# Pooled scores of one batch from every fourth column of q, and a rearranged start

## The chip, the cores and the metric

The kernel runs on one core of a Trainium2 chip. A core has five engines with a queue each: TensorE (PE in the profile; its weight loads are listed as PEld), VectorE (DVE), ScalarE (ACT), GpSimd (POOL) and SyncE (SP), which here issues nearly all DMAs. The engines run side by side and wait for each other through semaphores. Inputs and output lie in the chip's memory (HBM); work is done from an on-chip buffer, and matmul results arrive in an accumulation buffer, PSUM, of eight banks. The metric is the time of one execution in microseconds (us), as a median over runs. The profile is of one execution, and its span covers the instructions alone.

## The reference: what is computed

Shapes: q, k and v are 8 batches x 8 heads x 576 positions x 64. Two attentions are added, then a second block works on the result.

```python
q_d = q.reshape(B, H, Sd, 4, D).mean(axis=3)      # Sd = 144; k_d, v_d likewise
out_d = sm_attn(q_d, k_d, v_d)                    # softmax(q_d k_d' / 8) v_d
out_up = np.repeat(out_d, 4, axis=2)
scores = np.where(abs(i - j) < 4, scale * q @ k.T, -1e9)
out_local = softmax(scores) @ v
x = (out_up + out_local), heads side by side      # 576 x 512 per batch
theta = x @ w_theta
u = x + w_tok_r @ (x * cos(theta)) + w_tok_i @ (x * sin(theta))
return u + np.maximum(u @ w_ch, 0.0)
```

The pooled scores are the product of sums over four neighbouring positions of q and of k. Since the product is linear in q, the sum over the four positions of q may be taken before the product or after it.

## The kernel before

**One list of words sets the order.** `ORDER` is written out by hand: 1191 words, each one step of one batch (and of one part of it). The last loop reads the words in turn; the first two letters name the step, which takes the next item of its own list of batches and parts, and the rest names a place: an engine (v VectorE, a ScalarE, g GpSimd), a PSUM bank or pair of banks, or one of 16 staging buffers. `pin` ties every instruction to the one before it on its engine, so that each engine works strictly in the order of the words. Nothing is planned at run time: an engine waits at its next instruction until the data and the banks are there. While a batch is in its second block, the next batch's attention is already under way.

**The way of a batch**, with the two letters of the words. SyncE loads k and q (`lk`, `lq`, line 287) and casts bring them to bf16 (`ck`, `cq`, line 295). TensorE transposes them (`tp`, line 302) so that head dimensions lie on partitions, and `ev` (line 315) copies the result from PSUM to `kT` and `qT`. `kd` and `qd` (lines 319 to 336) sum four neighbouring columns: on VectorE one reduction (line 321), on GpSimd two additions (lines 329, 332 and 335). v comes in through `lv`, `lw`, `cv`; for batch 0 alone through whole loads, casts, transposes, copies and products with the identity (`l1`, `c1`, `t1`, `e1`, `x1`, lines 362 to 390). `pv` and `vd` make the pooled v. Then come two softmaxes side by side:

- the local one: scores of windows of 64 positions (`ps`, line 482), exponential (`ex`, 490), band mask (`mk`, 503 and 505), product with v (`po`, 515), division (`nm`, 523 and 524);
- the pooled one: scores (`sd`, line 426), exponential (`ed`, 437), product with the pooled v (`nd`, 447 and 452), division (`xn`, 457 and 458), transpose and copy (`xd`, `xc`).

`xt` transposes the local result, and `xa` (line 545) adds the two into `xT`. The second block takes `xT` through theta (`th`, line 556), sines (`cs`, 561 and 562), products (`zz`), the token mixing (`mx`, line 636, the largest piece of work), the sum (`ua`), and the channel product (`ch`, line 666) with its output (`rl`, `st`). The weights are loaded (`la`, `lb`, `lc`) and cast (`ca`, `cb`, `cc`) in between; the token weights are also transposed (`wp`, `wc`).

**The pooled scores.** `sd` fills a pair of banks in two parts of twelve matmuls each. In every one of them 64 head dimensions meet two groups of 32 pooled keys and 144 pooled queries: a 64x64 corner of the array, with 144 columns moving through it. The row half is the head's parity `par`, which also names the bank; the column half is `x`. The exponential `ed` scales by 1/8 and by 1/16, since both operands are sums of four and not means.

**Idle matmuls.** A word `wm` multiplies a buffer of zeros into a bank that nothing reads: the first figure after it is the bank, the second a count of 512-column matmuls, the third a last piece in units of 64 columns. Six more of 512 columns stand ahead of the list (line 226). In the part that is changed there are words of 7168, 1984, 960, 1088, 1280 and 2944 columns.

Of the kernel before, what the change touches and what calls it, by code (L numbers as in the profile page):

```python
# [15 lines left out]
B = 8  # L16
# [4 lines left out]
SD = S // 4  # L21
# [8 lines left out]
NCH = 5  # L30
# [9 lines left out]
HALF = 64  # L40
# [4 lines left out]

XDMA = (6, 7)
# [6 lines left out]
VT = (0,)  # L53
# [10 lines left out]
lv8 cbg wcv wcv wp1 zz zp7 tp45 cs qdg wp3 wp6 zz wcv lw zz wcv wcv zca eva wp7 wcv wp1 wca te wp0 wcv ps34 ps56 ex ex  # L64
ps12 mx0 lq1 cvg lk2 lka mx7 lqc mx3 qdv cvg ua lk7 ex ua lk0 mkv mkv kdg sd67 po45 nm sd12 lq4 cva lk5 lk9 cvg cvg ed
ed mx0 ua ua lq3 pv67 po45 po23 nm mx0 vda mkg nd67 lk8 nd45 lkb nm xn xn lq6 ckg ckg tp12 mx3 po45 ua lca ua nm cqg
cqg tp67 eva eva xd0 ckg ckg up1 lq7 po23 lvc xcv nm tp45 xt67 cqg mx0 cqg xt23 eva xt45 lv4 qdg kdg uca lw lv0 lw lw
lv3 lv1 lw lw xa xa tp67 cka ts ckg ckg th1 th2 xa th5 lk8 xm4 evv cs cqg xm1 ckv th3 zz tt4 up6 lq6 lqb cs zz tp12
xm7 ua cs ucv ct cs cqg eva te ztv xm6 zz zz mx0 ua tp34 zp7 tp56 ps12 zcv mx7 mx0 ex cvv kdg evv eva lk7 lk9 cvg lk4
qdg ua up7 uca sd12 mkv ps34 po56 ex ua ccv lcc lc5 kdg nm mkv mx0 sd34 ed po56 cvg cvg ua cqg mx7 nm ua ed mx0 ua lk2  # L70
# [30 lines left out]
def kernel(  # L101
# [11 lines left out]
    nc = tc.nc  # L113
# [28 lines left out]
    qT = tiles(2, [P, 4, S], "qT")  # L142
# [665 lines left out]
```

## Time and profile before

| | |
|---|---|
| median of 3 runs | 233.53 us (231.45, 233.53, 234.31) |
| profiled execution | 231.04 us |
| its span | 229.3 us, 9430 instructions |
| TensorE busy | 219.4 us, 96% of the span |
| VectorE, ScalarE, GpSimd busy | 187.8, 154.3 and 147.4 us |
| DMA, first 40 us | 11.62 MB, 291 GB/s on average |
| token mixing, line 636 | 576 matmuls, 78.1 us |
| pooled scores, line 426 | 192 matmuls, 5.6 us |
| idle matmuls of the list, line 764 | 32 matmuls, 9.9 us |
| pooled sums of q on GpSimd, first addition | 14 times, 16.5 us |

A row of the chain of waits gives start, length, engine, tile and line, and how many instructions are merged in it. A row of the timeline gives start, length, engine, line, operation, the tile written and the tiles read with their shapes, the count, and in brackets how long the engine stood idle before and what it waited for. In the row of the slices each digit is the busy share of one fortieth of the span, in tenths. A row of a group ends in its busy time, the mean of one instruction in ns, and the idle time ahead of it. The length of a matmul in a row holds its way through the array too; the pace of a series is read from the chain, where such overlap is taken out. A busy TensorE in the first 20 us is in part busy with idle matmuls.

### The profile page before, as it was taken

The page shows a single profiled execution, that of the slowest core. Times are in us where ns is not written, and L with a number is a line of the kernel's source. Part 1 is how long each engine was busy: PE and PEld are TensorE (multiplying, and loading weights), DVE is VectorE, ACT ScalarE, POOL GpSimd, SP SyncE. Part 2 cuts the span into 40 slices and gives each one's busy share as a digit, 9 for nine tenths or more (in the row PEclk, how much of TensorE's full clock was granted, in tenths as well). Part 3 has the DMA queues.
Part 4 walks back from the last instruction along what each step waited for, and adds up shares of the span by engine and source line. Part 5 has one row for each costly group of instructions (what it writes and reads, how often), then busy time and mean ns, then how long its engine had stood idle before and what let it go on. Part 6 is the DMA issues. An engine that isn't in the chain of part 4 may idle for free.

```text
span 229.3 us, 9430 instructions
## 1 busy us (share of the span) xinstructions
PE 219.4 (96%) x3970; PEld 152.3 (66%) x3970; DVE 187.8 (82%) x370; ACT 154.3 (67%) x240; POOL 147.4 (64%) x194
## 2 busy tenths in 40 slices
PE   7997899999999999999999999989998999999992
PEld 2475678776878666885785685766655775667741
DVE  6599998989988899889978798798986967648473
ACT  2279999689988999898888997868786132530000
POOL 7589998879996999997978399379933020200000
PEclk9999999999999999999999999999999999999999
DMA  6999987999998799979799996992473466655787
GB/s 180 394 390 390 294 176 212 370 326 174 319 336 162 196 297 265 203 163 284 157 261 353 270 146 175 136 131 77 90 152 84 71 139 186 139 146 132 152 223 268
DMA packets 76795, 49.41 MB, mean 216 GB/s; under 512 B 61136, under 2 KB 61392, under 8 KB 76752
## 3 DMA queue, kind: packets, MB, share of 16 engines
q1 hardware_dynamic: 76096, 47.76, 80.7%
q10 hardware_dynamic: 656, 1.05, 1.3%
q8 instruction: 31, 0.51, 1.0%
q14 instruction: 12, 0.10, 0.2%
HBM read 33.98 MB, written 9.44 MB: 189 GB/s over the span
## 4 chain that ended last, share of the span: by engine, by line
PE 75%; DVE 10%; DMA 5%; POOL 4%; issue 2%; ACT 2%; SPq 0%; DVEq 0%; POOLq 0%; ACTq 0%
PE PS L636 27%; PE PS L666 10%; PE PS L556 10%; PE PS L302 5%; DMA ur<-uT 4%; PE PS L515 2%; PE PS L537 2%; PE PS L595 2%; PE PS L764 2%; PE PS L482 2%; PE PS L568 2%; POOL two L329 1%; POOL pm L503 1%; PE PS L447 1%; DVE pm L505 1%
## 5 line engine op out<-in xcount | busy, mean ns | idle before, releaser
L636 PE MATMUL PS<-WT,z 128*128 128x288 bf16 x576 | 78.1, 286 | 0.0
L636 PEld LDWEIGHTS <-z 128*128 128x128 bf16 x576 | 53.9, 98 | 16.1 <-issue 1.3
L641 DVE TENSOR_TENSOR uT<-PS,xT 128x288 bf16<-128x288 f32 x64 | 28.5, 451 | 10.2 <-PE PS L636 9.4
L561 ACT ACTIVATE cs<-PS,pihc 128x512 bf16<-128x512 f32 x32 | 22.1, 690 | 21.0 <-PE PS L556 13.4
L556 PE MATMUL PS<-wth,xT 128*128 128x512 bf16 x128 | 32.1, 379 | 0.1
L666 PE MATMUL PS<-wch,uT 128*128 128x512 bf16 (+1 forms) x132 | 31.1, 373 | 0.0
L524 DVE TENSOR_TENSOR tmp<-PS,rl 128x512 bf16<-128x512 f32 x40 | 27.6, 691 | 1.4
L545 DVE TENSOR_TENSOR xT<-PS,xdT 128x928 bf16<-128x928 f32 (+1 forms) x24 | 22.3, 952 | 3.7 <-PE PS L537 3.6
L490 ACT ACTIVATE pm<-PS 128x1024 bf16<-128x1024 f32 (+1 forms) x24 | 20.5, 880 | 6.6 <-PE PS L482 5.4
L674 DVE SCALAR_TENSOR_TENSOR osb<-PS,ur 128x512 f32<-128x512 f32 x28 | 19.1, 685 | 6.7 <-DMA ur<-uT 3.9
L577 POOL TENSOR_TENSOR zT<-xT,cst 128x512 bf16<-128x512 bf16 x7 | 10.0, 1422 | 21.8 <-ACT cst L574 21.8
L295 POOL CAST k_tm<-st 128x576 bf16<-128x576 f32 x23 | 15.5, 691 | 7.6 <-DMA st<-in_k_dram 7.5
L770 ACT ACT_TABLE_LOAD x15 | 19.2, 1283 | 0.3
L666 PEld LDWEIGHTS <-uT 128*128 128x128 bf16 x132 | 11.9, 98 | 11.2
L295 POOL CAST q_tm<-st 128x576 bf16<-128x576 f32 x24 | 17.0, 725 | 3.3 <-DMA st<-in_q_dram 3.2
L562 ACT ACTIVATE cs<-PS 128x512 bf16<-128x512 f32 x32 | 19.1, 598 | 0.0
L396 POOL CAST v_w<-st 128x512 bf16<-128x512 f32 x21 | 13.4, 656 | 8.5 <-DMA st<-in_v_dram 8.5
L556 PEld LDWEIGHTS <-xT 128*128 128x128 bf16 x128 | 11.4, 98 | 10.3 <-DVE xT L545 0.7
L503 POOL TENSOR_TENSOR pm<-pm,band 128x512 bf16<-128x512 bf16 x16 | 18.1, 1158 | 0.0
L329 POOL TENSOR_TENSOR two<-qT 128x576 f32<-128x576 bf16 x14 | 16.5, 1177 | 1.5 <-ACT qT L315 1.2
L620 DVE TENSOR_TENSOR z<-PS,cs 128x1024 bf16<-128x1024 bf16 x24 | 15.8, 683 | 0.8 <-issue 0.4
L329 POOL TENSOR_TENSOR two<-kT 128x580 f32<-128x580 bf16 x13 | 15.0, 1154 | 0.4
(123 smaller groups left out, 421.5 us busy)
## 6 DMA issues: line engine op xcount, KB each, us to landing
st<-in_k_dram SPq DMA_DIRECT2D x32, 288.0 KB, 6.2
st<-in_q_dram SPq DMA_DIRECT2D x32, 288.0 KB, 5.8
st<-in_v_dram SPq DMA_DIRECT2D x70, 128.0 KB, 4.9
out_dram<-osb SPq DMA_DIRECT2D x26, 256.0 KB, 3.5
st<-in_v_dram SPq DMA_DIRECT2D x4, 288.0 KB, 3.0
st<-in_moe_w_tok_r_dram SPq DMA_DIRECT2D x4, 288.0 KB, 6.2
st<-in_moe_w_tok_i_dram SPq DMA_DIRECT2D x4, 288.0 KB, 6.0
st<-in_moe_w_theta_dram SPq DMA_DIRECT2D x4, 256.0 KB, 5.9
```

The costliest lines, as they stand in the source:

```text
L295: COPY[w](out=to, in_=of)
L329: nc.gpsimd.tensor_tensor(out=t, in0=src[:, :, 0:2], in1=src[:, :, 2:4], op=ALU.add)
L490: nc.scalar.activation(out=pm[(3 * b + u) % NPM][:, :, 0:n].rearrange("p e c j w -> p e (c j w)"), in_=at.pop(("ps", b, u))[:, :, 0:4 * W ...
L503: EW[w].tensor_tensor(out=t[:, x], in0=t[:, x], in1=m[:, x], op=ALU.mult)
L524: nc.vector.tensor_tensor(out=tmp[(NCH * b + c) % NTMP].rearrange("p g (j d) -> p g j d", d=D), in0=ps[:, :, :, 0:D], in1=r.unsqueeze(3).t ...
L545: nc.vector.tensor_tensor(out=xT[b % 2][:, :, lo:lo + cnt].rearrange("p e (m j) -> p e m j", j=4), in0=at.pop(("xt", b, u))[:, :, 0:cnt].r ...
L556: nc.tensor.matmul(out=ps, lhsT=xT[b % 2][:, dc, P * c:P * c + P], rhs=wth[:, dc, :], start=(dc == 0), stop=(dc == 3))
L561: nc.scalar.activation(out=t[:, 0, :], in_=ps, func=AF.Sin, bias=pihc, scale=1.0)
L636: nc.tensor.matmul(out=ps, lhsT=z[b % 2][:, j, P * dc:P * dc + P], rhs=WT[:, j, cols], start=(j == 0), stop=(j == 8))
L641: nc.vector.tensor_tensor(out=uT[b % 2][:, dc, cols], in0=at.pop(("mx", b, i)), in1=xT[b % 2][:, dc, cols], op=ALU.add)
L666: nc.tensor.matmul(out=ps[:, cols], lhsT=uT[b % 2][:, dc, P * c:P * c + P], rhs=wch[:, dc, cols], start=(dc == 0), stop=(dc == 3))
L770: nc.scalar.activation(out=idle, in_=pihc, func=TABLE[kind])
```

## The change

Three things change, all of them ahead of the first sines of batch 0; the last 1034 words are the same in the same order.

1. `QSUM = (0,)`: batch 0 has no `qd` steps (one on VectorE, one on GpSimd). Its `sd` takes `qT` itself: the 576 columns are seen as 144 groups of four, and four matmuls, each with every fourth column, starting at 0, 1, 2 and 3, add up in PSUM. A part has 48 matmuls instead of 12, each with its own weight load. Ahead of them the loop runs over the two row halves inside and over the four columns outside. The sum of q is no longer rounded to bf16 in between.
2. The first 157 words are rearranged and partly given to other engines. The loads of SyncE keep order and buffers. Two of batch 0's four value casts go from VectorE to GpSimd; one key cast goes from ScalarE to GpSimd, another from GpSimd to ScalarE, one query cast from GpSimd to VectorE; a value copy changes places with another between VectorE and ScalarE. The second pooled sum of k goes from VectorE to GpSimd, the copies of the pooled v from ScalarE to VectorE. On TensorE the first output step comes between the two parts of the pooled scores, and the third group of local scores behind both and behind the second output step. Of the weight and batch 1 casts six change engines. The 960 idle columns that stood ahead of batch 0's first query transposes stand behind batch 1's first key transposes.
3. The first idle word, 14 matmuls of 512 columns, becomes one of six and 64 words of one 64-column matmul each.

```diff
+QSUM = (0,)
...
 ORDER = """
-kcg l10 l11 l12 l13 kcv lk4 lq5 kcg kcv lk6 lk7 c1v c1g wm7e0 t101 c1v c1v t123 e1a e1v cka ckg wm737 tp01 ckg x12 x13
-lq8 x14 x15 cqg cva cva cqg lk9 ckg cva lqa wm717 tp67 evv x14 cqg lqb cqa tp01 cvv evv wm521 tp23 cva pv47 evv qdv
-kdg eva lk1 la3 ckg vda qdg wm624 ps01 ps23 kdv wm656 sd67 sd45 ex mkv la6 cag ex lq4 lq2 lk5 ed ed lk8 ckv ps01 lq9
-po23 nm cqg mkg po67 lba ex cba mkg cqa nd45 nd23 cag tp01 nm xn xn po67 po45 nm nm po23 nm eva xd0 lkb tp67 ckg lq7
-cka xca la1 eva cqg la0 cag cqg caa ts lb3 lb4 lb5 xt45 xt01 xt23 tp67 lbc lba lb2 lb8 xa lb1 cbg lv7 kdg th4 lw xa
-xm5 th0 lv0 lw lv3 lvb xa cbv cbg tt3 cs xm4 th2 zz evv cbg cs wp0 wp1 wp5 cbg cbg ct lw lw th3 wcv ztg cs cbg xm2 xm0
...
+wm760 wm701 wm701 wm701 wm701 wm701 wm701 wm701 wm701 wm701 wm701 wm701 wm701 wm701 wm701 wm701 wm701 wm701 wm701
+wm701 wm701 wm701 wm701 wm701 wm701 wm701 wm701 wm701 wm701 wm701 wm701 wm701 wm701 wm701 wm701 wm701 wm701 wm701
+wm701 wm701 wm701 wm701 wm701 wm701 wm701 wm701 wm701 wm701 wm701 wm701 wm701 wm701 wm701 wm701 wm701 wm701 wm701
+wm701 wm701 wm701 wm701 wm701 wm701 wm701 wm701 kcg l10 l11 kcv l12 c1v l13 c1g c1g kcg c1g lk4 t101 t123 kcv wm737
+lq5 ckg e1a cqv lk6 lk7 ckg lq8 e1v cqg tp01 cka x12 x13 x14 x15 evv cva lk9 ckg lqa tp67 cva cvv cva evv cqg tp01 evv
+lqb cqa x14 cva wm521 tp23 eva pv47 wm624 ps01 ex lk1 la3 la6 kdg ps23 ckg kdg ex wm656 cav vdv sd67 lq4 cqg lq2 lk5
+lk8 mkv po23 lq9 sd45 ed ckv nm po67 mkg nm lba cbg ps01 lkb ed ex nd45 nd23 mkg xn tp01 wm717 cqg cka lq7 xn caa po67
+po45 nm eva xd0 po23 la1 cka nm cqg xca la0 tp67 lb3 eva lb4 lb5 cqg xt45 xt01 nm xt23 cag xa lbc xa lba cbg tp67 cbv
+caa lb2 ts lb8 th4 xm5 kdg cbg lb1 lv7 lw lv0 xa lw cs lv3 cbv th0 lvb evv tt3 zz th2 xm4 cs wp0 wp1 wp5 cbg cbg ct lw
+lw th3 wcv ztg cs cbg xm2 xm0 lv8 cbg wcv wcv wp1 zz zp7 tp45 cs qdg wp3 wp6 zz wcv lw zz wcv wcv zca eva wp7 wcv wp1
...
@@ -421,10 +425,18 @@
         ps = at["sd", b, part] = pair(w)
 
         def mm(blk, g, x, col):
-            for par in range(2):
-                r = slice(HALF * par, HALF * par + HALF)
-                nc.tensor.matmul(out=ps[HALF * x:HALF * x + HALF, par, SD * col:SD * col + SD],
-                                 lhsT=kd[b % 2][r, blk, g:g + 2, :], rhs=qd[b % 2][r, blk, :], start=True, stop=True)
+            r = [slice(HALF * par, HALF * par + HALF) for par in range(2)]
+            if b in QSUM:
+                quads = qT[b % 2][:, blk, :].rearrange("p (m j) -> p m j", j=4)
+                rhs = [[quads[r[par], :, j] for j in range(4)] for par in range(2)]
+            else:
+                rhs = [[qd[b % 2][r[par], blk, :]] for par in range(2)]
+            n = len(rhs[0])
+            for j in range(n):
+                for par in range(2):
+                    nc.tensor.matmul(out=ps[HALF * x:HALF * x + HALF, par, SD * col:SD * col + SD],
+                                     lhsT=kd[b % 2][r[par], blk, g:g + 2, :], rhs=rhs[par][j],
+                                     start=(j == 0), stop=(j == n - 1))
 
         for blk in ((0, 1, 2) if part == 0 else (3,)):
...
-        kd=(kdf, span(B, 2)), qd=(qdf, span(B, 2)), lv=(lv, [(b, c) for b, c in span(B, NCH) if b not in VT]), lw=(lw, [(b, c) for b, c in span(B, NCH) if b not in VT]),
+        kd=(kdf, span(B, 2)), qd=(qdf, [x for x in span(B, 2) if x[0] not in QSUM]), lv=(lv, [(b, c) for b, c in span(B, NCH) if b not in VT]), lw=(lw, [(b, c) for b, c in span(B, NCH) if b not in VT]),
```

More of the change, by code (lines that the diff above doesn't have):

```diff
@@ new lines @@
+sd12 lq4 cva lk5 lk9 cvg cvg ed ed mx0 ua ua lq3 pv67 po45 po23 nm mx0 vda mkg nd67 lk8 nd45 lkb nm xn xn lq6 ckg ckg
+tp12 mx3 po45 ua lca ua nm cqg cqg tp67 eva eva xd0 ckg ckg up1 lq7 po23 lvc xcv nm tp45 xt67 cqg mx0 cqg xt23 eva
+xt45 lv4 qdg kdg uca lw lv0 lw lw lv3 lv1 lw lw xa xa tp67 cka ts ckg ckg th1 th2 xa th5 lk8 xm4 evv cs cqg xm1 ckv
+th3 zz tt4 up6 lq6 lqb cs zz tp12 xm7 ua cs ucv ct cs cqg eva te ztv xm6 zz zz mx0 ua tp34 zp7 tp56 ps12 zcv mx7 mx0
+ex cvv kdg evv eva lk7 lk9 cvg lk4 qdg ua up7 uca sd12 mkv ps34 po56 ex ua ccv lcc lc5 kdg nm mkv mx0 sd34 ed po56 cvg
@@ new lines @@
+lv3 mx5 zca sd67 lw ps01 ex po34 mx2 ua lw ed tp01 sd67 cva nm po34 eva cvv cvg ed lw up5 uca ua mx2 cvg nm cvg lvc
+xd3 ua pv04 xcv lk7 lk0 mx7 lq9 lq6 lq2 lqd lq8 lqb lq5 ckg ckg vda lq7 lw xt56 mkv cqg cqg po34 lk4 xt01 xa xa ch2 st
+cva ts lv6 th5 up6 ckg xm0 nm th1 tp34 cs ucv cs mkg rl eva mx6 ua ua th1 xt67 lk0 lk1 cs cqa po45 mkv xa nm ht3 rt
+tp67 th1 eva zz xm2 lv9 xm3 xm4 lw lve zz zz ckg dk4 kdv mx0 cqg tp67 nd23 xn cs zz ua cqa eva mx1 nd67 xn cqa sr cqa
+cka tt2 ct dkb up4 cva cva ua mx0 mx7 ua cvg cvv uca te po01 nm qdg kdg qdg sd56 ed po23 ua ch4 rl xd0 ch1 ztg lw nm
@@ L97 @@
+du du st uta dt sta rl st rl ht7 ch2 sta rl st rl sta rl st rt ssa sr rl sta rm su k0
 """
```

54 lines of the change are left out of this document (21 added, 33 removed).

## The prediction

> **What bounds the kernel now.** I read the page first (span, slices, chain), then the chain of waits in order of time up to 36 us, then the timeline of each engine there, because the change ends at the first sine of batch 0, near 29 us.
>
> ```profile
> span 229.3 us, 9430 instructions
> PE   7997899999999999999999999989998999999992
> PE 75%; DVE 10%; DMA 5%; POOL 4%; issue 2%; ACT 2%; SPq 0%; DVEq 0%; POOLq 0%; ACTq 0%
> ```
>
> TensorE (PE) carries three quarters of the chain. After the fifth slice it hardly has a hole, so what the first 28 us gain or lose is handed on: later words are the same in the same order, and each engine works in order. The start itself is no TensorE stage. The next rows, of the chain, give start, length and work:
>
> ```profile
> 4.00 4.54 PE PS L764 x14
> 8.54 0.52 PE PS L376 x9
> 9.08 1.12 ACT xT L379
> 10.20 0.58 ACT k_tm L295
> 10.91 0.68 PE PS L302 x9
> ...
> 13.64 1.36 DVE qT L315
> 15.00 1.27 DVE kT L315
> ...
> 17.46 0.36 ACT vd L415
> 17.85 1.03 ACT pm L490
> 18.91 0.95 DVE pm L505
> ...
> 26.38 1.13 DVE xT L545
> 27.55 1.04 PE PS L556 x4
> ```
>
> The chain hands over between idle matmuls, casts, evacuations and the two softmaxes; theta of batch 0 starts at 27.55. That is the point to be moved. From there the chain is gapless TensorE work, so I take its shift as the shift of the end.
>
> **Part by part: the idle matmuls.** Fourteen of 512 columns become six and 64 of 64: the same 7168 columns, 56 more matmuls.
>
> ```profile
> 6.35 0.15 PEld L764 LDWEIGHTS <-warm 128*128 128x128 bf16 x1 [0.28 <-issue]
> 6.78 1.26 PEld L764 LDWEIGHTS <-warm 128*128 128x128 bf16 x6 [0.28 <-issue]
> 182.55 0.47 PE PS L568 x16
> ```
>
> Up to 6.78 one starts each 0.43 us; then six weight loads fit in 1.26 (0.21 each): TensorE runs at half its rate until 6.8. The nearest row to a 64-column piece is L568, 128x128 weights too: 0.47/16 = 29 ns. Six whole ones end at 4.00+6x0.43 = 6.58, three pieces at twice 29 ns reach 6.78, the other 61 take 61x29 ns = 1.77: end 8.55 against 8.54. Worth nothing.
>
> **The first casts.** The order moves two of batch 0's value casts from VectorE (DVE) to GpSimd (POOL), and swaps keys and queries among the engines.
>
> ```profile
> 5.85 1.98 DVE L371 CAST z<-st 128x512 bf16<-128x512 f32 x6
> 6.45 0.88 POOL L371 CAST z<-st 128x576 bf16<-128x576 f32 x1
> 3.14 0.43 SPq L287 DMA_DIRECT2D st<-in_q_dram  x1
> 6.37 1.25 SPq L287 DMA_DIRECT2D st<-in_q_dram  x2
> st<-in_q_dram SPq DMA_DIRECT2D x10, 288.0 KB, 5.8
> 9.52 1.43 POOL L295 CAST k_tm<-st 128x576 bf16<-128x576 f32 x2 [2.20 <-DMA st<-in_k_dram]
> ```
>
> GpSimd's three casts end at 6.45+3x0.88 = 9.1 at the latest (a constant ahead of them now stands between them): just in time for the second transpose group, whose first one still runs from 8.55 to 9.05. VectorE takes the first query block, which lands at 3.14+5.8 = 8.95; a cast (1.98/3 = 0.66) later, 9.6, it evacuates the second value group, 1.36 by the query row above: 10.95, as before. So the first 9.6 us stay. The gain begins here: ScalarE (ACT) did a key cast (0.58) after its evacuation on which the first key transposes waited; now both blocks come from GpSimd, the second landing at 9.52 and cast by 10.15. The evacuation ends at 10.2, the 1984 idle columns behind the transposes (0.83 us at 0.21 per 512) near 10.4, so the key transposes start at 10.4, not 10.91: 0.5 gained.
>
> ```profile
> 13.92 0.68 PE L302 MATMUL PS<-ident,k_tm 128*128 128x128 bf16 x9
> 14.89 0.67 PE L302 MATMUL PS<-ident,q_tm 128*128 128x128 bf16 x9
> 15.60 1.12 ACT L315 COPY qT<-PS 128x1152 bf16<-128x1152 bf16 x1 [0.99 <-PE PS L302]
> ```
>
> Without the 960 idle columns between them (0.40 us), and with the value cast that frees bank 4 moved from ScalarE's third place to VectorE behind the first evacuation (10.95+1.3+0.65 = 12.9), the third group starts behind that evacuation and the queries' transposes, near 12.65, the fourth behind 1088 idle columns (0.45) near 13.9. The last is held by the fourth query block: issued second in the 6.37 row, about 7.3, +5.8 = 13.1, cast 0.69. VectorE's two evacuations then end at 14.2 and 15.5 (before 15.00 and 16.27), ScalarE's runs 14.5 to 15.6 (before to 16.72). Gain 0.8 to 1.1.
>
> **No sums of q.**
>
> ```profile
> 16.18 1.34 DVE L321 TENSOR_REDUCE qd<-qT 128x288 bf16<-128x1152 bf16 x1
> 17.44 1.35 DVE L321 TENSOR_REDUCE kd<-kT 128x290 bf16<-128x1160 bf16 x1
> 16.86 1.15 POOL L329 TENSOR_TENSOR two<-qT 128x576 f32<-128x576 bf16 x1 [0.99 <-ACT qT L315]
> 18.08 0.67 POOL L335 TENSOR_TENSOR qd<-two 128x288 bf16<-128x288 f32 x1
> 17.35 1.42 PE L764 MATMUL PS<-warm 128*128 128x512 bf16 x6
> 18.70 0.59 PE L426 MATMUL PS<-qd,kd 64*64 64x144 bf16 x24
> ```
>
> VectorE loses 17.44+1.35-16.18 = 2.6 us and receives a theta-weight cast (0.62 by its ScalarE row below) and the pooled values' copies (on ScalarE from 16.72 to 17.82, taken alike): 15.5 to 17.2. GpSimd does the keys' second sum where it did q's: 1.9 us from 15.5 to 17.4, before 18.79 on VectorE. ScalarE's first exponential no longer stands behind the pooled values: the scores ended 0.65 behind the evacuation (16.72 to the filler at 17.35), now 15.6 to 16.3, so the exponential begins near 16.1 instead of 17.85, the mask at 17.2 instead of 18.91. Late next is TensorE's own filler: 2944 columns, 1.23 us, behind the scores at 16.3, so the pooled scores start near 17.6 instead of 18.70. Lead: 1.1 us. SyncE's loads keep their order and buffers; only who frees a buffer changes, and the one freed later (by the cast of batch 1's first query block, from ScalarE to GpSimd behind the masks) holds a token-weight load that no step before theta needs.
>
> **What is added.** Each pooled score becomes four accumulating matmuls: 48 per part instead of 12.
>
> ```profile
> 97.00 0.38 PE PS L426 x24
> L426 PEld LDWEIGHTS <-kd 64*64 64x64 bf16 x192 | 3.3, 106 | 2.2 <-issue 1.7 <-ACT pm L490 0.2
> ```
>
> 24 took 0.38 us, 16 ns each, with four 64x64 corners of the array in turn: 63 ns per matmul of one corner, weights included. The new inner loop stays on one column half and alternates two row halves, so I take a pair per 63 ns: 24x63 = 1.5 us per part, a little less where one half takes over from the other: 1.4. Lower end 48x16 = 0.76 (all four corners stay busy); upper end 48x63 = 3.0 (no overlap, or the every-fourth-column read at half rate; no row here reads columns apart). I stay near the row's own pace because its pairs differ only in the corner.
>
> [...]
>
> **What is late next.**
>
> ```profile
> 20.66 0.69 DVE L524 TENSOR_TENSOR tmp<-PS,rl 128x512 bf16<-128x512 f32 x1
> 19.67 1.68 ACT L437 ACTIVATE pd<-PS 128x864 bf16<-128x864 f32 x2
> 21.21 0.63 ACT L490 ACTIVATE pm<-PS 128x512 bf16<-128x512 f32 x1
> 23.13 1.12 ACT L315 COPY kT<-PS 128x1152 bf16<-128x1152 bf16 x1 [0.17 <-PE PS L302]
> 26.55 0.62 ACT L243 CAST wth<-st 128x512 bf16<-128x512 f32 x1
> ```
>
> Pooled scores 17.6 to 19.0; first output 19.0 to 19.3; second part 19.3 to 20.6; its exponential 20.75 to 21.6 (before 20.5 to 21.35); the last mask group's exponential 21.6 to 22.2, before 21.21 to 21.84. So ScalarE is 0.35 behind, and its next six (two casts, the evacuation, cast, pooled copy, evacuation, the last theta weights) are as many as before: the weights at 26.95 to 27.6. VectorE runs its seven normalisations (0.85 each): four before xn's end at 23.9, then three to 26.45, so xT from 26.45, 0.07 late. The 960 idle columns moved before the third output cost 0.40 on TensorE, from 22.75 to 23.15, under VectorE's queue; without that cover 0.40. Theta needs both, 27.6 to 27.8 against 27.55. Sum: lead -1.1, two parts 2x(1.4-0.3) = +2.2, and about -0.8 of waits in which TensorE stood idle for exponentials and masks: +0.3. With a part at 1.2, -0.1; with more queueing, +0.9.
>
> **Against its own time.** The profiled execution took 231.04 us: forecast 231.3 there. The three other times (231.45, 233.53, 234.31) make the median 233.53, 2.5 us above it; the mean of the four is 232.6, and I put the new median at 232.6+0.3 = 232.9. Chance 0.62.
>
> **Rivals.**
>
> - All four corners overlap, 16 ns each: a part is 0.76, the pooled exponentials end 1.3 earlier, theta starts near 26.5: -1.0, 230.0 in the profile, 231.6 as median. For it: L426's pace. Against: two corners per pair. Chance 0.14.
> - Slower, by pairs that do not overlap: a part of 3.0 us where strided columns or accumulation serialise the pair. Pooled scores end 17.6+3.0+0.2+3.0 = 23.8, 3.2 behind the forecast: +3.5, 234.5 in the profile, 236.1 as median. It decides against the change above 1.25 us per part, where the lead is used up. Chance 0.08. [...]
> - Loads not hidden: 63+106 ns per pair, 24x169 = 4.1 us per part, +2.7 each: +5.7, 236.7 and 238.3. Chance 0.02.
> - The pieces do not lift the half rate: 64x58 ns = 3.7, to 10.3 instead of 8.55. Of these 1.75 some 0.6 disappears in waits for queries: with the forecast's +0.3 it is +1.5, 232.5 and 234.1. For it: with whole ones the rate rose only at 6.78. Chance 0.06.
> - It does not do what it says: blocks land later than the median row, and the 1.1 lead is gone while the added matmuls stay: +1.4, 232.4 and 234.0. Chance 0.08.
>
> **Numbers.** Forecast alone, -0.1 to +0.9 on readings from 231.0 to 234.3: 230.9 to 235.2. Rivals one, four and five fall inside; left out are the two slow ones and odd readings. 2% is about 4.7 us, roughly what a measurement of this kernel can tell from no change: only unhidden loads or a serial pair on a slow reading pass it, 0.04 slower; 0.03 faster for scatter and the first rival; 0.93 within.
>
> **What would show it.** Pooled scores starting near 17.6 and a part of 1.2 to 1.5 prove both terms; near 0.8 or 3.0 the rivals. Value transposes after 9 us show the pieces. Theta before 26.9 or after 28.7 makes the prediction wrong, as does an end that does not follow theta's shift.

## The result, and the profile after

| | before | after |
|---|---|---|
| median (six runs each, measured together) | 231.58 us (229.9 to 234.31) | 234.0 us (233.2 to 236.05) |
| profiled execution | 231.04 us | 235.18 us |
| its span | 229.3 us | 233.5 us |
| pooled scores of batch 0 start | 18.70 us | 17.98 us |
| theta of batch 0 starts | 27.55 us | 31.87 us |

After over before is 1.0124, with a 95% interval of 1.0083 to 1.0164: slower by 1.2%, less than 2% and yet clearly more than nothing. The ratios here and below leave out executions that are more than 1.5% above the fastest of the same kernel, so they are not quite the quotients of the medians. The forecast was no change (+0.3 us).

The page of the changed kernel: the span, the engines' busy time and counts, TensorE's slices, the clock granted to it in tenths, the chain by engine, and the queue named "instruction".

```profile
span 233.5 us, 9656 instructions
PE 220.6 (94%) x4070; PEld 156.5 (67%) x4098; DVE 187.6 (80%) x370; ACT 153.3 (66%) x237; POOL 146.6 (63%) x193
PE   7997699999999999999999999999999999999992
PEclk9999979999999999999999999999999999999999
q8 instruction: 32, 0.52, 1.0%
PE 84%; DMA 4%; DVE 4%; issue 3%; SPq 1%; ACT 1%; POOL 0%; DVEq 0%
```

TensorE has a deeper dip in its fifth slice (6 tenths, before 8), and its clock one in the sixth. "issue", in which an engine waits for nothing that the profile shows, grew from 2% to 3% of the chain. The chain of waits of the changed kernel (start, length, what) says where:

```profile
10.37 0.68 PE PS L306 x9
...
15.93 0.77 PE PS L494 x56
16.70 0.16 issue
16.86 1.19 PE PS L776 x5
18.05 1.68 PE PS L437 x48
19.73 0.13 PE PS L527 x16
19.86 1.01 PE PS L437 x30
20.87 1.34 issue
22.21 0.84 PE PS L437 x18
...
27.32 0.15 PE PS L527 x3
27.48 0.93 issue
28.40 0.31 PE PS L527 x13
...
30.53 1.12 PE PS L306 x9
31.65 0.22 issue
31.87 1.22 PE PS L568 x3
```

The start went nearly as forecast: key transposes at 10.37 (10.4 forecast), pooled scores (L437) at 18.0 (17.6). Then two holes stand in the middle of words. TensorE stops after 30 of the 48 matmuls of the second part of the pooled scores for 1.34 us, and after three of the sixteen matmuls of the third output word (L527) for 0.93 us. No buffer or bank is waited for: the matmuls on both sides of a hole read and write the same tiles. Theta comes 4.32 us later than before, and the span is 4.2 longer: the end followed theta's shift, as the prediction had assumed. (These two executions lie 4.1 us apart and the ratio is worth 2.9: the profiled execution of the changed kernel is the second longest of its six.) The windows of the changed kernel (busy time of each engine and count, then granted clock, DMA share, GB/s) show a second thing:

```profile
20.00:25.00 5.00, 2.93 (x102) 2.62 (x93) 2.00 (x5) 2.63 (x5) 2.22 (x4) 1.00 1.06 334
25.00:30.00 5.00, 3.65 (x136) 2.92 (x137) 4.00 (x9) 3.43 (x6) 4.92 (x8) 0.93 0.76 210
30.00:35.00 5.00, 4.78 (x79) 3.29 (x73) 4.99 (x7) 4.36 (x8) 2.36 (x4) 0.73 0.76 186
```

After the holes TensorE was granted 0.93 and 0.73 of its clock; before had 1.00 in the same three. Nine transposes (L306 at 30.53) then take 1.12 us instead of the 0.68 of the row at 10.37.

**The place of the holes.** Each matmul is two instructions on TensorE, a weight load and a multiply. Counted in the program, the first instruction behind the first hole is number 701 of TensorE, and the first behind the second is number 957: 256 apart. The queue named "instruction" moved 32 packets of together 0.52 MB, 16 KB each. TensorE's 4098 loads, each with its multiply (28 multiplies have no record), are 8196 instructions, 256 per packet; the kernel before has 31 packets for 2 x 3970 instructions, again 256. So I read the holes as blocks of 256 instructions that came late. The change adds 56 matmuls in the idle pieces and 72 in the pooled scores: 2 x 128 = 256 instructions, one whole block, all ahead of theta.

The packets can be found in time. The DMA view of 19.7 to 20.7 us and that of 25.5 to 26.5 us of the changed kernel hold one each (count, MB, share of the engines' time):

```profile
q8 instruction: 1, 0.02, 6.8%
```

```profile
q8 instruction: 1, 0.02, 8.2%
```

By its records the second packet began at 25.65 and ended at 26.97, and instruction 957 ran at 28.40. TensorE had entered the block ahead of it, at number 701, at 22.21. So 3.4 us passed until the packet moved, it took 1.3, and TensorE went on 1.4 later. The first packet (19.8 to 20.9) belongs to the entry into number 445 at 16.25 and to instruction 701 at 22.21: 3.6, 1.1 and 1.3. So in this execution some six microseconds passed from entering one block to running the next, and where TensorE was through a block sooner, it stood. The theory to be tested is that instructions that come late make the loss. The rivals: the pooled-score part was mispriced (1.68 us and not 1.4) and the corners of the array decide it; or the clock is lost by itself, and the holes matter little.

### The profile page after: what moved, and what is told of

The parts are those of the page before. It is cut to its first block, busy times and chain, and to the rows that moved or that the text cites. A ratio compares the mean times of both kernels' runs of the same rounds, so it can differ in the third digit from the quotient of the medians.

```text
span 233.5 us, 9656 instructions
## 1 busy us (share of the span) xinstructions
PE 220.6 (94%) x4070; PEld 156.5 (67%) x4098; DVE 187.6 (80%) x370; ACT 153.3 (66%) x237; POOL 146.6 (63%) x193
## 4 chain that ended last, share of the span: by engine, by line
PE 84%; DMA 4%; DVE 4%; issue 3%; SPq 1%; ACT 1%; POOL 0%; DVEq 0%
PE PS L648 29%; PE PS L568 11%; PE PS L678 11%; PE PS L306 7%; PE PS L527 3%; PE PS L494 3%; PE PS L549 3%; DMA st<-in_k_dram 3%; PE PS L437 3%; PE PS L607 2%; PE PS L459 2%; DMA ur<-uT 2%; PE PS L580 2%; PE PS L464 2%; DVE pm L517 2%
## 5 line engine op out<-in xcount | busy, mean ns | idle before, releaser
L653 DVE TENSOR_TENSOR uT<-PS,xT 128x288 bf16<-128x288 f32 x64 | 28.5, 452 | 12.2 <-PE PS L648 10.2
L568 PE MATMUL PS<-wth,xT 128*128 128x512 bf16 x116 | 31.0, 384 | 0.7 <-issue 0.2
L678 PE MATMUL PS<-wch,uT 128*128 128x512 bf16 (+1 forms) x122 | 29.8, 373 | 0.9 <-issue 0.6
L299 POOL CAST q_tm<-st 128x576 bf16<-128x576 f32 x24 | 16.2, 692 | 6.4 <-DMA st<-in_q_dram 6.3
L449 ACT ACTIVATE pd<-PS 128x864 bf16<-128x864 f32 x16 | 13.9, 887 | 5.5 <-PE PS L437 5.5
L333 POOL TENSOR_TENSOR two<-kT 128x580 f32<-128x580 bf16 x14 | 16.3, 1162 | 0.7 <-ACT kT L319 0.3
L333 POOL TENSOR_TENSOR two<-qT 128x576 f32<-128x576 bf16 x13 | 15.3, 1179 | 2.1 <-ACT qT L319 1.8
```

The costliest lines, as they stand in the source:

```text
L299: COPY[w](out=to, in_=of)
L333: nc.gpsimd.tensor_tensor(out=t, in0=src[:, :, 0:2], in1=src[:, :, 2:4], op=ALU.add)
L568: nc.tensor.matmul(out=ps, lhsT=xT[b % 2][:, dc, P * c:P * c + P], rhs=wth[:, dc, :], start=(dc == 0), stop=(dc == 3))
L653: nc.vector.tensor_tensor(out=uT[b % 2][:, dc, cols], in0=at.pop(("mx", b, i)), in1=xT[b % 2][:, dc, cols], op=ALU.add)
L678: nc.tensor.matmul(out=ps[:, cols], lhsT=uT[b % 2][:, dc, P * c:P * c + P], rhs=wch[:, dc, cols], start=(dc == 0), stop=(dc == 3))
```

## Experiments

**Whole idle matmuls.** The changed kernel with fourteen whole matmuls again: 112 instructions fewer, so that number 701 lies elsewhere.

```diff
-wm760 wm701 wm701 wm701
...
-wm701 kcg l10 l11 kcv
+wm7e0 kcg l10 l11 kcv
```

> The changed kernel with its first idle word whole again (14 matmuls of 512 columns; 112 fewer instructions on TensorE ahead of everything else). In the trace of the changed kernel TensorE stands still, waiting for nothing that the profile shows, for 1.34 us ahead of its instruction 701 (the weight load of the 79th pooled-score matmul) and for 0.93 us ahead of instruction 957 (the fourth matmul of the third output group), 256 apart. Theory 'fetch': instructions come in blocks of 256, each asked for when the one before is entered and there some 5.5 us later, so the stalls stay at 701 and 957, which are now other steps: 701 is in the second pooled output (nd, about 24.3 us, stall about 1.6), 957 in the third group of local transposes (xt, about 30 us, stall about 1.5); the pooled scores run unbroken. Theta of batch 0 starts at 31.0 to 32.0 (31.87 with the pieces, 27.55 before); time 0 to 1 us off the changed kernel's. Theory 'pieces' (the small idle matmuls themselves cost time): theta near 28.5 and about 2.5 us faster than the changed kernel. Theory 'pooled scores' (their own 1.7 us per part and what follows them make the loss): stalls stay where they are in the work, at the second part of the pooled scores; theta as with the pieces.

Measured: median 233.28 us, ratio 1.0078 [1.0034, 1.0122], theta at 29.77. The timeline of TensorE in this kernel (start, length, line, tiles, count, idle before):

```profile
19.17 1.80 PE L434 MATMUL PS<-qT,kd 64*64 64x144 bf16 x48
...
23.44 0.26 PE L456 MATMUL PS<-vd,pd 128*72 128x65 bf16 x2 [1.12 <-issue]
...
28.54 0.56 PE L546 MATMUL PS<-ident,tmp 64*64 64x58 bf16 x46 [0.53 <-issue]
```

The second part of the pooled scores is now unbroken, and the holes stand where 701 and 957 fell, in the pooled product and in the transposes of the local result. That is the sharpest evidence: a hole that moves by instruction count, and not with a tile. Theta came 1.2 earlier than the earliest expected, since the second hole was 0.53 and the clock stayed at 1.00.

**Four corners in turn.** The changed kernel with the loops turned: two column halves and two row halves within each of the four strided columns.

```diff
+        def mms(group):
...
             for j in range(n):
-                for par in range(2):
+                for blk, g, x, col in group:
+                    for par in range(2):
...
-            for x in range(2):
-                mm(blk, 2 * x, x, blk % 3)
+            mms([(blk, 2 * x, x, blk % 3) for x in range(2)])
```

> The changed kernel with the loops of the pooled scores turned: for each of the four columns the matmuls of both column halves and both row halves follow each other, so that all four corners of the array are in turn; as many instructions as before, in the same places but for their order within a block of scores. All theories: a part takes about 0.8 to 0.9 us instead of 1.68. Theory 'fetch': instruction 701 is reached at about 19.2 instead of 20.9, but is not there before about 22.2, so the stall grows to about 2.7 us and all that follows stays where it was: theta within 0.4 us of 31.87, time within 0.3% of the changed kernel. Theory 'pooled scores': theta 1.5 to 1.7 us earlier, time 0.7% less.

Measured: 234.55 us, 1.0126 [1.0062, 1.0191]. The chain of this kernel:

```profile
19.29 1.67 PE PS L437 x48
20.96 0.13 PE PS L526 x16
21.09 1.03 PE PS L437 x30
22.12 0.90 issue
23.02 0.84 PE PS L437 x18
```

The part is 1.67, the same as with two corners, though all four are now in turn. No theory had that: the order of the corners is not what makes 35 ns per matmul (1.67/48). The hole is at the same matmul, 0.90 long where 'fetch' expected 2.7 after a shorter part. A query block landed late in this execution, so everything in it is about 1.2 later; its theta (32.56) is not compared.

**The pieces alone.** The kernel before with only its first idle word cut into six whole ones and 64 pieces: 112 instructions more, with no idle column more.

```diff
-c1v c1g wm7e0 t101 c1v c1v t123
+c1v c1g wm760 wm701 wm701 wm701
...
+wm701 t101 c1v c1v t123
```

> The kernel before with only its first idle word changed to six whole matmuls and 64 pieces of 64 columns: the same columns, 112 more instructions on TensorE ahead of the first transposes. Theory 'fetch': the block limits at 445, 701 and 957 now fall into the local scores (16.7 us), the second pooled output (22.3) and the third local transposes (due near 26); the last block is not there before 28, a stall of 1 to 2 us ahead of instruction 957, theta at 28.5 to 29.5 instead of 27.55, time 1 to 2 us more than before. Theory 'pooled scores' and every theory in which only the work counts: the idle matmuls end at 8.5 as before, theta at 27.5, time as before. Theory 'pieces cost time themselves': value transposes later than 8.6.

Measured: 233.45 us, 1.0064 [1.0019, 1.0109]. The timeline of TensorE:

```profile
22.62 0.42 PE L455 MATMUL PS<-vd,pd 128*72 128x130 bf16 x4 [0.32 <-issue]
...
28.00 0.43 PE L540 MATMUL PS<-ident,tmp 64*64 64x58 bf16 x30 [1.66 <-issue]
```

Theta is at 29.16, 1.6 late, though the pooled scores start at 18.64, where they did before. Pieces that are idle work of the same length cost 0.6% by their number alone. (The profiled execution took 236.01 us, 2.6 above its own median; only its first 35 us are read here, and the length of its holes is not set against the 0.6%.)

**Lighter loads.** If a block's packet waits behind the loads of data, fewer loads bring it sooner. The changed kernel loads 144 of the 576 columns of each token weight and copies them four times over, so the token mixing works with other weights.

```diff
-            nc.sync.dma_start(out=t, in_=moe_w_tok_r[P * i:P * i + P, :])
+            nc.sync.dma_start(out=t[:, 0:144], in_=moe_w_tok_r[P * i:P * i + P, 0:144])
-        COPY[w](out=to, in_=at.pop(("wtok", i)))
+        COPY[w](out=to.rearrange("p (a c) -> p a c", a=4),
+                in_=at.pop(("wtok", i))[:, 0:144].unsqueeze(1).to_broadcast([P, 4, 144]))
```

> The changed kernel with the loads of the token weights cut to their first 144 of 576 columns (the casts read those four times over, so that the token mixing works with wrong weights; this part of the computation is changed). About 2 MB less is moved between 18 and 30 us; the instructions of TensorE are the same. Theory 'fetch, slowed by the loads beside it': the block that holds 957 is asked for at 22 and is there sooner than 5.5 us later: the stall ahead of 957 (0.93) is gone, the one ahead of 701 (1.34) stays or shrinks, theta at 30 to 31 instead of 31.87. Theory 'fetch takes the same time whatever else is moved': both stalls as in the changed kernel, theta within 0.3 of 31.87. Theory 'pooled scores': no change of the stalls either.

Measured: 232.83 us, 1.0061 [1.0019, 1.0103], theta at 29.87. The windows of this kernel:

```profile
20.00:25.00 5.00, 3.54 (x113) 3.22 (x104) 2.49 (x6) 3.24 (x5) 2.81 (x4) 1.00 0.52 166
25.00:30.00 5.00, 4.01 (x161) 3.18 (x160) 4.86 (x11) 4.55 (x7) 4.92 (x9) 1.00 0.19 49
```

The hole at 701 shrank to 0.74, the one at 957 is gone, and the clock stays at 1.00. The packet for 957 began at 22.97, 1.3 us after number 701 ran (21.69), where it had been 3.4: the loads were dying down by then (143 GB/s from 21.7 to 23.0, against 289 from 22.2 to 25.6 with full loads). For 701 the block ahead was entered at 16.33, when the loads still ran at 387 GB/s (from 15 to 20), and the packet waited 2.8. So about two of the six microseconds, 3.4 less 1.3, are a wait that goes with the loads of data.

**Neighbouring columns.** The next question was the 35 ns. The kernel with whole idle matmuls, but each of the four matmuls reads 144 columns that lie side by side; the pooled scores of batch 0 are then sums over other positions of q.

```diff
-                quads = qT[b % 2][:, blk, :].rearrange("p (m j) -> p m j", j=4)
+                quads = qT[b % 2][:, blk, :].rearrange("p (j m) -> p m j", j=4)
```

> The changed kernel with its first idle word whole and with the four matmuls of a pooled score taking 144 neighbouring columns of q each instead of every fourth (the pooled scores of batch 0 come out of other sums; this part of the computation is changed). Matmuls, weights, order and instructions are those of the run with the whole idle word, where a part of the pooled scores took 1.68 us, 35 ns per matmul, and turning the loops over all four corners of the array left that as it was. Theory 'stride' (reading every fourth column holds each half of the rows at one stream at a time): two corners at full pace, 30 to 33 ns per matmul, 1.45 to 1.6 us per part. Theory 'adding' (matmuls that add to the same bank follow each other at this pace): 1.68 us. This run alone hardly tells the two apart, its companion with turned loops does. Theta of batch 0 as in the run with the whole idle word, 29.5 to 30.

The same with the four corners in turn:

> As the run before (144 neighbouring columns, first idle word whole; this part of the computation is changed), with the loops turned so that all four corners of the array are in turn. Theory 'stride': 16 to 18 ns per matmul as in the kernel before, 0.75 to 0.9 us per part. Theory 'adding': 35 ns, 1.68 us per part, as with every fourth column. In both theories instruction 701 is the same block limit: with shorter parts TensorE comes to it about 1.6 us sooner and waits that much longer if the block is late, so theta stays between 29 and 30 although 1.6 us of matmul time are gone.

Measured in one run each: 234.04 and 234.98 us. A part took about 1.0 us in the first (21 ns a matmul) and, by the chain of the second, this:

```profile
17.90 0.93 PE PS L434 x48
18.83 0.02 issue
18.86 1.78 ACT pd L445 x2
20.63 0.04 issue
20.68 0.36 PE PS L455 x6
21.04 3.62 issue
24.66 0.26 PE PS L455 x2
```

19 ns a matmul: reading every fourth column cost the other 14 to 16, whichever corners are used. 21 ns in the first run is less than any theory there had; in the second 'stride' holds and 'adding' does not. And it gained nothing. TensorE was through its block earlier and stood 3.62 us at number 701 (2.18 in the first, theta at 31.30), and theta is at 32.05. Both thetas are later than the expected 29 to 30, and both executions lost clock (0.67 granted from 25 to 30 in the second; in the first nine transposes took 1.16 us from 25.33, where the run with whole idle matmuls has 0.66). Nearly half of the part's length was taken away, and in these two executions, one of each kernel, the wait for the instructions, and the clock lost behind it, took it back and more.

**The order alone.** The new order with the sums of q restored in both the list and the words of batch 0, and whole idle matmuls. It has the instruction count of before.

```diff
-QSUM = (0,)
+QSUM = ()
...
-pv47 wm624 ps01 ex lk1 la3 la6 kdg ps23 ckg kdg ex wm656 cav vdv sd67
+pv47 wm624 qdv ps01 vda ex lk1 la3 la6 kdg ps23 ckg qdg kdv ex wm656 cag sd67
```

> The new order of the first words without the other two parts: sums of q restored for batch 0 (one on VectorE, one on GpSimd, with the second key sum back on VectorE, the pooled values' copies back on ScalarE, one theta cast on GpSimd, since the sums of q need the place), first idle word whole. TensorE has as many instructions as the kernel before. Theory 'fetch' (blocks of 256 instructions, about 5.5 us from the entry of one block to the presence of the next): limits at 445 and 701 fall into the first and third output groups; nothing is due much before its block; pooled scores near 18.0 to 18.3, theta at 26.8 to 27.6, time 0 to 0.4% less than before. Theory 'the new order itself costs' (moved casts, the third score group late): theta later than 28 and time at least 0.4% more than before.

Measured: 231.21 us against 231.63, 0.9989 [0.9953, 1.0025]; theta at 26.90, 0.65 earlier than before, with a hole of 0.38 ahead of 701 and none ahead of 957. (Another idle time of 0.38 stands ahead of number 949, where the matmul next to it waits for VectorE's `xT`; it is no late block.) The new order is harmless, and its lead of 0.65 us does not stand clear of the noise in the medians.

**The pooled scores alone.** The kernel before, with four matmuls for each pooled score of batch 0 and without its two sums of q.

```diff
+QSUM = (0,)
-pv47 evv qdv kdg eva lk1 la3 ckg vda qdg wm624
+pv47 evv kdg eva lk1 la3 ckg vda wm624
```

> The kernel before with the sums of q of batch 0 left out and its pooled scores taken by fours, and no other change: 144 more instructions on TensorE, all of them in the pooled scores, 2.6 us less on VectorE, 1.9 less on GpSimd. Theory 'fetch': the limit at 445 is reached at 18.9 as before; 701 is now in the second pooled output and is there only at 24.2 to 24.5, a stall of about 1 us; 957 in the local transposes about 30; theta at 30 to 31.5, time 1 to 1.6% more than before. Theory 'matmul time alone': two parts at 1.68 instead of about 0.3 minus idle time, theta at 29 to 29.5, time 0.5 to 0.8% more.

Measured: 234.7 us, 1.0151 [1.0108, 1.0193]. The timeline of TensorE:

```profile
18.42 3.33 PE L434 MATMUL PS<-qT,kd 64*64 64x144 bf16 x96
...
24.25 0.33 PE L456 MATMUL PS<-vd,pd 128*72 128x65 bf16 x4 [1.18 <-issue]
```

In the old order the pooled scores hardly start earlier (18.42 against 18.70), the 96 matmuls take 3.33 us where 24 took 0.59, a hole follows, and then the clock: 0.55 granted from 25 to 30. Theta is at 30.93, as 'fetch' had it (30 to 31.5; 'matmul time alone' had 29 to 29.5). Of the three parts this one loses most, and in it the longer series (2.74 us more) is a larger piece than the hole (1.18).

**Whole idle matmuls and light loads together.** Meant to leave only the pooled scores' own time.

```diff
-wm760 wm701 wm701 wm701
...
+wm7e0 kcg l10 l11 kcv
...
-            nc.sync.dma_start(out=t, in_=moe_w_tok_r[P * i:P * i + P, :])
+            nc.sync.dma_start(out=t[:, 0:144], in_=moe_w_tok_r[P * i:P * i + P, 0:144])
```

> The changed kernel with its first idle word whole and with the token-weight loads cut to a quarter (their first 144 columns, read four times over by the casts: the token mixing works with wrong weights, this part of the computation is changed). With the whole word alone TensorE stood 1.12 us ahead of instruction 701 and 0.53 ahead of 957, and theta of batch 0 started at 29.77. Theory 'fetch, slowed by the loads beside it': 957 comes without a stall, 701 with 0.5 to 1.1 (the block limit 445 lies near 18.2 and the cut loads leave the queues only from 19 on); theta at 28.3 to 29.2; against the kernel before with the same cut loads (its companion) +0.4 to +0.8%. Theory 'pooled scores and order' (the stalls are a symptom): theta stays at 29.5 to 30.

Measured: 233.76 us against 232.23, 1.0055 [1.0008, 1.0101]. Against its companion, the kernel before with the same light loads (the next experiment, 231.38 us), it is 1.0% longer by the medians, where 0.4 to 0.8 was expected. So a good part of the loss is there without a hole at 957 and with the clock at 1.00. Theta at 30.08 missed what 'fetch' had (28.3 to 29.2) and lies next to the rival's 29.5 to 30: the pooled scores began at 18.40, 0.9 later than with full loads, and 0.87 of hole stayed at 701. From pooled scores to theta it is 11.68, against 8.85 before: 0.87 of hole and 1.96 more of work and waits. The forecast's step had 1.35 more; with 2x0.28 for the longer parts it is 1.91, so without late instructions the step's working nearly holds.

**Light loads in the kernel before.**

```diff
-            nc.sync.dma_start(out=t, in_=moe_w_tok_r[P * i:P * i + P, :])
+            nc.sync.dma_start(out=t[:, 0:144], in_=moe_w_tok_r[P * i:P * i + P, 0:144])
```

> The kernel before with the token-weight loads cut to a quarter in the same way (this part of the computation is changed): what the lighter loads give by themselves. In the kernel before TensorE stands 0.17 us ahead of instruction 957, and its third output group, in which 701 falls, takes 0.47 instead of 0.32 us. Theory 'fetch': both go, theta at 27.1 to 27.5 instead of 27.55, time 0 to 0.4% less. Theory 'loads bound the start': theta 1 us or more earlier.

Measured: 231.38 us, 0.9973 [0.9932, 1.0014], and 8.86 from pooled scores to theta. (Theta is at 26.95, a little earlier than expected, because the pooled scores began 0.61 earlier.) Lighter loads gain nothing clear of the noise here, where no instruction is late ahead of theta; in the changed kernel they brought theta 2.0 us forward (31.87 to 29.87). The ratios, 1.0124 and 1.0061, point the same way, but their intervals overlap.

**A shorter idle word.** The order alone, with seven idle matmuls instead of fourteen, 14 instructions fewer.

```diff
-wm7e0 kcg l10 l11 kcv
+wm770 kcg l10 l11 kcv
```

> The new order with the sums of q restored, and the first idle word cut from 14 to 7 whole matmuls: 14 instructions fewer ahead of everything else, and TensorE idle for up to 1.5 us before the value transposes. With 14 it stood 0.38 us ahead of 701 and 0.38 ahead of 957, and theta started at 26.90. Theory 'fetch': the limits move seven matmuls on, the two stalls shrink to 0.2 to 0.35, theta within 0.3 of 26.9, time as before or up to 0.5% less. If the rate of the matmuls falls back for want of idle work, transposes take 1.1 instead of 0.67 us after 8 us, and theta is later than 27.5.

Measured: 231.91 us, 1.0042 [1.0004, 1.0079]; theta at 27.47, 0.27 later than expected, and the time 0.4% more where none or less was expected; clock at 1.00. The hole at 701 is 0.31, as expected. The 0.38 that the expectation puts ahead of 957 is the wait for `xT` at number 949, and its fate tells the two kinds of hole apart: it now stands ahead of number 935, 14 lower, since 14 instructions are left out. A wait for data stays with its step; a late block stays with its number. Nothing is gained by shortening the idle start.

**No idle words.** To part the holes from the clock: the kernel before without its three idle words ahead of the pooled scores. No instruction is late here.

```diff
-cvv evv wm521 tp23 cva pv47 evv qdv
-kdg eva lk1 la3 ckg vda qdg wm624 ps01 ps23 kdv wm656 sd67
+cvv evv tp23 cva pv47 evv qdv
+kdg eva lk1 la3 ckg vda qdg ps01 ps23 kdv sd67
```

> The kernel before without the three idle words around the first local and pooled scores (1088, 1280 and 2944 columns, 24 instructions): TensorE then stands idle there for some 2.5 us in gaps of up to 1.3 us, between 14 and 19 us, without any late block. It asks whether such gaps alone bring the half rate that was seen behind the late blocks (transposes of 9 in 1.1 us, theta's matmuls 0.43 apart). Theory 'idle time lowers the rate': matmuls at half rate somewhere between 17 and 28 us, theta 0.5 to 1.5 us later than 27.55, time up to 0.6% more. Theory 'the rate falls only with late blocks': full rate throughout, theta within 0.4 of 27.55, time as before.

Measured: 233.24 us against 231.4, 1.0079 [1.004, 1.0119], a little more than the 0.6% expected; theta at 28.83, within the first theory's range. The timeline of TensorE and then the windows of this kernel:

```profile
16.04 0.94 PE L482 MATMUL PS<-qT,kT 64*64 64x64 bf16 x64 [0.48 <-DVE kT L315]
17.30 0.46 PE L426 MATMUL PS<-qd,kd 64*64 64x144 bf16 x8 [0.32 <-DVE qd L321]
18.57 0.44 PE L426 MATMUL PS<-qd,kd 64*64 64x144 bf16 x16 [0.82 <-DVE kd L321]
```

```profile
15.00:20.00 5.00, 2.95 (x129) 1.96 (x127) 5.00 (x5) 4.81 (x7) 4.73 (x7) 0.90 1.05 389
20.00:25.00 5.00, 4.19 (x97) 3.95 (x97) 4.06 (x11) 3.58 (x7) 5.00 (x7) 0.50 1.04 345
25.00:30.00 5.00, 4.88 (x112) 4.01 (x112) 4.47 (x8) 4.40 (x7) 4.92 (x9) 0.58 1.07 268
```

Ordinary waits of 0.48, 0.32 and 0.82 us, close together, were followed by a granted clock of 0.50 and 0.58 in the last two rows. By the shares in the three rows I estimate some 10 us at half clock, from about 19.0. So clock is lost here with no late instruction; that the holes of the changed kernel cost it its clock as idle time is my reading. How much idle time it takes is not settled: in the run with whole idle matmuls and light loads 0.73 and 0.87 us, ending at 22.88 and 24.11, left the clock at 1.00, and in the run with the shorter idle word 1.32, 1.08 and 0.59 us, ending at 6.87, 8.62 and 10.73, left the next nine transposes at 0.68 us.

**The holes side by side.** From the timelines and the windows; "added" counts TensorE's instructions against before, and theta is its start. With four corners in the changed kernel, and in the first run with neighbouring columns, the loss of clock is read from nine transposes of 1.16 us, at 26.26 and 25.33.

| kernel | added | hole at 701 | hole at 957 | clock below 0.95 | theta |
|---|---|---|---|---|---|
| before | 0 | none | 0.17 | no | 27.55 |
| changed | 256 | 1.34 | 0.93 | yes | 31.87 |
| changed, four corners | 256 | 0.90 | none | yes | 32.56 |
| changed, whole idle matmuls | 144 | 1.12 | 0.53 | no | 29.77 |
| before, pieces alone | 112 | 0.32 | 1.66 | yes | 29.16 |
| changed, light loads | 256 | 0.74 | none | no | 29.87 |
| whole idle matmuls, light loads | 144 | 0.87 | none | no | 30.08 |
| neighbouring columns | 144 | 2.18 | none | yes | 31.30 |
| neighbouring columns, four corners | 144 | 3.62 | none | yes | 32.05 |
| pooled scores alone | 144 | 1.18 | none | yes | 30.93 |
| order alone | 0 | 0.38 | none | no | 26.90 |
| order alone, shorter idle word | -14 | 0.31 | none | no | 27.47 |
| before, light loads | 0 | none | none | no | 26.95 |
| before, no idle words | -24 | none | none | yes | 28.83 |

None of these beats before by more than its interval. At all fifteen holes of the table TensorE went on 1.3 to 1.6 us after the packet of its block had ended, 5.1 to 6.5 us after it had entered the block ahead; and in none of the fourteen traces did it run the first instruction of a block sooner than 1.26 us after the end of its packet. This ties the holes to the packets in time, as their numbers tie them by place.

## Why the prediction was wrong

**What bounds the kernel: right in its frame.** The end followed theta (+4.2 for +4.32), and the first 28 us decided. In other pairs of profiles the two shifts fit less well (light loads in the kernel before: theta 0.6 earlier, span 1.5 longer), so later stages scatter too.

**Idle pieces, "worth nothing": wrong.** In engine time they cost nothing: by the timelines the stretch with one weight load each 0.43 us ended at 5.44 in this execution (before 6.78), and the first value transposes began at 7.74 (before 8.37). But they are 112 more instructions ahead of theta, and alone they cost 0.6%.

**First casts, and no sums of q: right, with a smaller lead.** Key transposes at 10.37 (10.4). The scores ended at 16.7 instead of 16.3, and then GpSimd was late, as two rows of the changed kernel's timeline show, first of GpSimd and then of the weight loads that waited:

```profile
15.79 1.29 POOL L333 TENSOR_TENSOR two<-kT 128x580 f32<-128x580 bf16 x1
17.16 0.67 POOL L336 TENSOR_TENSOR kd<-two 128x290 bf16<-128x290 f32 x1
```

```profile
17.98 1.45 PEld L437 LDWEIGHTS <-kd 64*64 64x64 bf16 x48 [0.37 <-POOL kd L336]
```

The second sum of k ended at 17.83, where 17.4 was forecast. The lead was 0.72 and not 1.1.

**What is added: mis-sized.** 1.68 per part instead of 1.4, inside the bounds of 0.76 and 3.0. The reason given, two corners per pair, was wrong: four corners took 1.67, and neighbouring columns 0.93 to 1.0. It is the read of every fourth column, which no row of before shows: 35 ns with a stride of four, 19 to 21 without. The third rival's 169 ns a pair did not come: a pair took 70 (2x35), and with neighbouring columns and four corners a load and its matmul took 19 ns together, where the record of one load is 106 ns long on average in before (L426) and 110 in the changed kernel (L437). So the loads did not stand one by one between the matmuls.

**What is late next: the step that failed.** It looked for the next late engine, bank or buffer, and took for granted that an instruction is there when its engine is free. From pooled scores to theta it had 10.2 us (17.6 to 27.8). Measured were 13.89: 10.2 + 2x0.28 for the two parts + 1.34 + 0.93 for the holes, and a remainder of 0.86, which I put down to the halved clock (the transposes at 30.53 alone lost 0.44); that share is argued and not measured. With 0.38 of later start that is theta's 31.87. The missing term is 2.27 us of late instructions and what they brought on. Three kernels with the changed pooled scores kept their clock ahead of theta, and in them the step less its holes comes out near the forecast's 10.2 + 0.56 = 10.76: 10.64 with whole idle matmuls (12.29 less 1.65), 11.07 with light loads (11.81 less 0.74), 10.81 with both (11.68 less 0.87). So the rest of the step, with its estimate of -0.8 for waits, held.

The sign could have been seen. Before's own weight loads have a small hole, by its timeline:

```profile
29.30 0.40 PEld L568 LDWEIGHTS <-wth 128*128 128x128 bf16 x5
29.87 0.38 PEld L568 LDWEIGHTS <-wth 128*128 128x128 bf16 x11 [0.17 <-issue]
```

A word of sixteen equal loads is split by 0.17 us that nothing explains, and that is number 957: there before already ran at the pace of its instructions, and 256 more ahead of it had to be paid for.

**The rivals.** None named this. The nearest, "it does not do what it says" (+1.4), had another cause; "pieces do not lift the half rate" had the right part with the wrong reason. The limit named there, theta after 28.7, was passed. The median of 234.0 lies in the range of 230.9 to 235.2 by luck: the kernel before, whose first three times gave 233.53, has a median of 231.58 over six, and the change cost about 2.9 us by the ratio where +0.3 was forecast.

**What stays open.** How the 2.9 us divide between holes, the longer pooled scores and the clock: the clock is lost in some profiled executions of these kernels and not in others, and each was profiled once. The mean clock on record for each of the changed kernel's six executions narrows it: the three with 0.997 or more took 233.2 to 233.83 us, the three with 0.993 or less 234.16 to 236.05. So against 231.58 about 2 us stay where little or no clock was lost. Starts differ by about 1 us between executions (pooled scores at 17.47 and at 18.40 with the same words, in the two runs with whole idle matmuls), so single profiles part effects of a microsecond only by place and count, not by time alone. That a packet waits while data is loaded fits its delays of 3.4 and 1.3 us; what makes it wait was not tested.

## What to carry to other kernels

Count instructions, not only busy time: where a change adds many short matmuls to a stretch in which loads run, look at how long TensorE takes for each 256 of its instructions, and set it against the 5.1 to 6.5 us per block that passed at the holes of this case. A hole marked "issue" inside a series of equal instructions was the sign here; find its instruction number and see whether the next one is 256 further on, and whether the matmul beside it waits for data. Here, replacing one engine's small sum by four times as many matmuls cost their own longer time and the wait for their instructions.

## What the runs showed of the hardware

- TensorE's instructions came in blocks of 256, one packet of 16 KB each (31 packets for 7940 before, 32 for 8196 in the changed kernel). The four packets timed here for numbers 701 and 957, in the changed kernel with full and with light loads, moved 1.3 to 3.6 us after the block ahead of theirs had been entered. From entry to use: 6.0 and 6.2 us at the holes of the changed kernel, with 3.4 to 3.6 us until the packet moved, 1.1 to 1.3 of transfer and 1.3 to 1.4 until it ran; with lighter loads, 1.3 us until one moved. At all fifteen holes it was 5.1 to 6.5 us.
- A matmul of a 64x64 corner over 144 columns: 35 ns with every fourth column, 19 to 21 ns with neighbouring ones, in both orders of the corners that were run.
- Three idle times of 0.48, 0.32 and 0.82 us within 3 us were followed by a granted clock of 0.50 from 20 to 25 us, in the kernel before without three of its idle words.
